# Recurrence, router and experts: experts on gathered rows of 128 in place of all tokens

## The chip, the cores and the metric

The kernel runs on one core of one Trainium2 chip, all in fp32. The time is the device time of one execution in microseconds, as the median of several runs. The engines are TensorE (PE; its weight loads are shown apart as PEld), VectorE (DVE), ScalarE (ACT), GpSimd (POOL) and SyncE (SP); DMAs are issued from SP's and POOL's queues. Each engine works through its own instructions in order.

## What is computed

```python
# hgrn2: 4 batches, 8 heads, 768 steps, head_dim 48
f = 1.0 / (1.0 + np.exp(-f_logit))
for t in range(S):
    state = f[:, :, t, :, None] * state + np.einsum('bhd,bhe->bhde', k[:, :, t], v[:, :, t])
    y[:, :, t] = np.einsum('bhd,bhde->bhe', q[:, :, t], state)
x = y.transpose(0, 2, 1, 3).reshape(B * S, H * D)          # 3072 tokens x 384
# router and experts: N, D, E, F = 3072, 384, 8, 1024
noisy_logits = x @ w_gate + np.log1p(np.exp(x @ w_noise)) * noise
top2 = np.argpartition(-noisy_logits, 2, axis=1)[:, :2]
...                                                         # top2_w: softmax of the two logits
for e in range(E):
    for k in range(2):
        mask = top2[:, k] == e
        h = np.maximum(x[mask] @ w1[e], 0.0)
        out[mask] += top2_w[mask, k, None] * (h @ w2[e])
```

Each of the 3072 tokens passes a linear recurrence, then a noisy router that picks 2 of 8 experts, and gets the weighted sum of those two experts' outputs.

## The kernel before

The sequence is cut into 6 stages of 128 steps; a stage has 4 chunks, one for each batch. `chunk` computes one: it transposes f, q and k (fp, qp, kp in L133), forms the diagonal of the attention-like matrix A (diag, L156), and goes through 7 levels. On each level PE computes scores sc (L172), DVE copies them under a mask into A (L178) and scales q (L182), and POOL scales k (kQ, L184) and forms the next decay factors T (L186); the next level's sc needs both. Then y comes from A and v (L193) and from q and the state (L197), is copied to yT (L200), and the state is renewed (kp L207, ds L214). Two chunks run in alternation, two such pairs per stage. The masks of the levels are built by POOL at the start (L91 to L96).

After a stage, `pack` re-arranges yT into xT with 10 DMAs on SP's queue (L232). `route` then computes the logits lg on PE (L244, 12 matmuls) and from them, with small operations of ACT and DVE (L249 to L272), one gate for every token and expert, which is zero for the experts that were not chosen. `expert` takes one expert and the 512 tokens of a stage, whatever the router chose: hp = w1 times xT (L295, 24 matmuls of 128x512), a ReLU on ACT (L297), yp = h times w2 (L303, 32 matmuls of 128x384), and DVE adds gate times yp to an accumulator in SBUF (L309). The last expert sends it out (L311). A matmul in fp32 shows as two records in the trace.

There are 48 pairs of expert and stage. Expert 0 on the stage before is woven into stages 1 to 5, with its instructions between the chunks' levels; the other 43 run after the last stage, expert by expert, with the weights loaded once for each expert in four DMAs of 768 KB on POOL's queue (L279, L284).

The order on each engine is made by a scheduler from the order in which the program is written and from the buffers' dependences; an engine that waits in its order holds all that stands behind.

## Time and profile before

| | us |
|---|---|
| median of 3 runs (2459.79 to 2460.49) | 2460.19 |
| span of the profiled execution | 2455.0 |
| PE busy | 2401.2 (98%) |
| DVE busy | 406.7 (17%) |
| ACT busy | 342.7 (14%) |
| POOL busy | 223.7 (9%) |

The profiled execution has the span given here; the median holds 5.2 us more, which lie around the span. Busy shares are averages over the whole span; a chain of waits tells which of the work sets the end, and the windows tell how the stages differ.

### The profile page before, as it was taken

The numbers are of one execution on the slowest core, as the hardware profiler recorded it, in microseconds if no ns is written. First come the engines' busy times: TensorE is split into PE (matmuls) and PEld (weight loads), VectorE is DVE, ScalarE is ACT, GpSimd is POOL, SyncE is SP. The second block draws the span as 40 slices with busy tenths as digits, with TensorE's granted clock in tenths as the row PEclk, the third lists the DMA queues.
The fourth block names the chain that finished last, engine by engine and source line by source line (L and its number), as shares of the span: only waits on it lengthen the run. The fifth ranks groups of instructions, "written<-read, shape, count | busy, mean of one in ns | idle before, by whom it ended". The sixth has DMA issues, their size and how long they took to land.

```text
span 2455.0 us, 23370 instructions
## 1 busy us (share of the span) xinstructions
PE 2401.2 (98%) x9984; PEld 1351.6 (55%) x9984; DVE 406.7 (17%) x777; ACT 342.7 (14%) x572; POOL 223.7 (9%) x397
## 2 busy tenths in 40 slices
PE   6999999999999999999999999999999999999999
PEld 5756666666655555555555555555555555555554
DVE  4534444443300000000000000000000000000000
ACT  1212121212120101111111111111111010101010
POOL 8322222221100000000000000000000000000000
PEclk9897979888799999999999999999999999999999
DMA  7412121211010001000100010001000100000000
GB/s 137 66 27 40 27 40 27 40 27 33 11 55 1 0 0 52 0 0 1 52 0 1 0 52 0 1 0 52 1 0 0 52 0 0 0 26 13 26 13 26
DMA packets 113255, 55.11 MB, mean 22 GB/s; under 512 B 101792, under 2 KB 104960, under 8 KB 113152
## 3 DMA queue, kind: packets, MB, share of 16 engines
q1 hardware_dynamic: 106560, 28.32, 6.8%
q0 software_dynamic: 6592, 25.29, 3.1%
q8 instruction: 79, 1.29, 0.2%
q14 instruction: 24, 0.20, 0.0%
HBM read 44.16 MB, written 4.72 MB: 20 GB/s over the span
## 4 chain that ended last, share of the span: by engine, by line
PE 95%; POOL 2%; ACT 1%; DVE 1%; issue 1%; DMA 0%; SPq 0%; ACTq 0%; DVEq 0%; POOLq 0%
PE hp L295 41%; PE yp L303 41%; PE sc L172 6%; PE y L193 2%; PE y L197 2%; PE diag L156 1%; PE lg L244 1%; PE ds L214 1%; PE fp L133 1%; PE kp L207 1%; POOL mf L94 0%; POOL mf L92 0%; PE qp L133 0%; PE kp L133 0%; DVE qP L182 0%
## 5 line engine op out<-in xcount | busy, mean ns | idle before, releaser
L295 PE MATMUL hp<-xT,w 128*128 128x512 f32 x2304 | 1016.0, 598 | 0.0
L303 PE MATMUL yp<-w,h 128*128 128x384 f32 x3072 | 1004.3, 487 | 0.0
L303 PEld LDWEIGHTS yp<-w,h 128*128 128x128 f32 x3072 | 581.6, 190 | 412.0 <-issue 21.5
L295 PEld LDWEIGHTS hp<-xT,w 128*128 128x128 f32 x2304 | 436.7, 191 | 525.6 <-issue 511.5
L297 ACT ACTIVATE h<-hp 128x512 f32<-128x512 f32 x384 | 229.3, 597 | 1672.6 <-PE hp L295 1672.6
L309 DVE SCALAR_TENSOR_TENSOR acc<-yp,gate,acc 128x384 f32<-128x384 f32 x168 | 103.8, 618 | 1628.3 <-PE yp L303 1628.3
L172 PEld LDWEIGHTS sc<-qP,kQ 48*128 48x128 f32 (+1 forms) x2688 | 185.1, 220 | 60.1 <-issue 34.3
L172 PE MATMUL sc<-qP,kQ 48*128 48x64 f32 (+1 forms) x2688 | 197.0, 309 | 19.2 <-POOL kQ L184 12.9
L178 DVE COPY_PREDICATED A<-masks,sc 128x512 f32<-128x512 uint8 x144 | 130.0, 903 | 94.3 <-PE sc L172 80.7
L279 POOL DMA_DIRECT2D w<-in_moe_w_dram x16 | 12.2, 765 | 1383.2 <-PE hp L295 1383.2
L184 POOL TENSOR_TENSOR kQ<-kQ,T 128x256 f32<-128x256 f32 x140 | 95.2, 681 | 199.3 <-PE sc L172 198.7
L182 DVE TENSOR_TENSOR qP<-qP,T 128x256 f32<-128x256 f32 x144 | 71.5, 496 | 18.0 <-PE sc L172 17.6
L193 PE MATMUL y<-A,v 128*48 128x128 f32 x384 | 50.5, 369 | 0.0
L180 ACT COPY A<-sc 64x512 f32<-64x512 f32 x24 | 13.4, 579 | 230.6 <-DVE qP L182 225.6
L197 PE MATMUL y<-qP,st 48*48 48x128 f32 x320 | 43.5, 360 | 0.0
L156 PE MATMUL diag<-qT,kQ 48*128 48x128 f32 x384 | 33.0, 306 | 9.3 <-ACT kQ L144 9.3
L186 POOL TENSOR_TENSOR T<-T 128x128 f32<-128x128 f32 (+4 forms) x140 | 36.6, 262 | 10.0
L156 PEld LDWEIGHTS diag<-qT,kQ 48*128 48x128 f32 x384 | 26.8, 201 | 16.0 <-ACT kQ L144 15.4
L193 PEld LDWEIGHTS y<-A,v 128*48 128x48 f32 x384 | 22.4, 154 | 23.7 <-issue 22.7
L158 DVE TENSOR_TENSOR A<-diag,ident 128x1024 f32<-128x1024 f32 x24 | 29.3, 1221 | 18.0 <-PE diag L156 18.0
L200 DVE COPY yT<-y 48x512 f32<-48x512 f32 x24 | 16.7, 695 | 89.2 <-ACT yT L200 89.2
L186 POOL TENSOR_TENSOR T<-f 128x256 f32<-128x256 f32 x24 | 14.7, 614 | 174.8 <-ACT f L137 174.7
(66 smaller groups left out, 468.0 us busy)
## 6 DMA issues: line engine op xcount, KB each, us to landing
w<-in_moe_w_dram POOLq DMA_DIRECT2D x32, 768.0 KB, 4.9
f<-in_f_logit_dram SPq DMA_DIRECT2D x24, 192.0 KB, 4.4
q<-in_q_dram SPq DMA_DIRECT2D x24, 192.0 KB, 5.0
k<-in_k_dram SPq DMA_DIRECT2D x24, 192.0 KB, 4.8
v<-in_v_dram SPq DMA_DIRECT2D x24, 192.0 KB, 3.3
out_dram<-acc SPq DMA_DIRECT2D x24, 192.0 KB, 1.9
xT<-yT SPq DMA_DIRECT2D x36, 96.0 KB, 2.4
xT<-yT SPq DMA_DIRECT2D x12, 64.0 KB, 2.0
```

The source lines that it names most:

```text
L156: nc.tensor.matmul(sc[:, par, cols(hp)], lhsT=kQ[rows(par), cols(hp)], rhs=qT[rows(par), cols(hp)], start=True, stop=True)
L172: nc.tensor.matmul(sc[0:nj, par, hp * HC:(hp + 1) * HC].rearrange("j (a m) -> j a m", m=m), lhsT=kQ[rows(par), hp * C:hp * C + nj], rhs=qv ...
L178: nc.vector.copy_predicated(Av, masks[:, l].rearrange("j (r x m) -> j r x m", r=2, m=m), scv)
L182: nc.vector.tensor_tensor(qv, qv, Tv[:, :, 0:1].broadcast_to((128, x, m)), ALU.mult)
L184: nc.gpsimd.tensor_tensor(kv, kv, Tv[:, :, 1:2].broadcast_to((128, x, m)), ALU.mult)
L186: nc.gpsimd.tensor_tensor(Tn, Tv[:, :, 0], Tv[:, :, 1], ALU.mult)
L193: nc.tensor.matmul(y[rows(par), par, cols(hp)], lhsT=vt[:, 2 * hp + par, :], rhs=A[:, par, cols(hp)], start=True, stop=(c == 0))
L197: nc.tensor.matmul(y[rows(par), par, cols(hp)], lhsT=state[b][rows(par), hp, :], rhs=qP[rows(par), cols(hp)], start=False, stop=True)
L295: nc.tensor.matmul(hp, lhsT=w[:, i, o:o + 128], rhs=xT[c][:, i, :], start=(i == 0), stop=(i == KO - 1))
L297: nc.scalar.activation(hs, hp, AF.Relu)
L303: nc.tensor.matmul(yp[:, 0:DM], lhsT=h[fo][:, b * C:(b + 1) * C], rhs=w2[fo // HALF][:, fo % HALF, :], start=(fo == 0), stop=(fo == FO - 1))
L309: nc.vector.scalar_tensor_tensor(a, in0=yp[:, 0:DM], scalar=g, in1=a, op0=ALU.mult, op1=ALU.add)
```

## The change

The router picks as before. Now the gates and the rows of x go to DRAM: the chunk transposes y to rows (xp, 4 transposes per chunk), and `route` writes them with the 8 gates as rows of 392 numbers to `xd` by 4 DMAs on SP's queue. `pack` is gone; lg reads yT itself (16 matmuls). A matmul pair rk with a triangle of ones counts for every chosen pair how many tokens have gone to the same expert before. From this DVE works out a place in a list per expert, and 8 indirect DMAs on POOL's queue scatter the token numbers into the lists `ids` in DRAM. `choose` decides on DVE, with some 35 small operations, which expert each of the next blocks belongs to; 55 blocks of 128 rows (LIST per stage, 22 of them after the last stage) hold all cases of 6144 chosen pairs. With the reference's inputs 52 of the 55 have rows.

`fetch` loads a block's 128 token numbers (`places`) on SP's queue, then its expert's weights in two DMAs of 1.57 MB whose address and condition come from registers (they are skipped if the buffer holds that expert), and gathers the rows of x with an indirect DMA on POOL's queue. There are three buffers of each. `block` transposes the rows (bx), computes bh (24 matmuls of 128x128), two ReLUs and by (8 matmuls of 128x384). POOL gathers the block's rows of the output, DVE adds gate times by, and POOL scatters the rows back. `clear` fills `ids`, `xd` and the output in DRAM at the start with 9 DMAs on POOL's queue, some 9.5 MB. `weave` puts the blocks of the stages before between the levels of stages 2 to 5.

The core of the diff:

```diff
...
+    LIST = [0, 9, 8, 8, 8, 22]
+    FIRST = [0, 0, 5, 0, 4, 0]
...
+    def clear():
+        nc.gpsimd.dma_start(out=ids.rearrange("(p r) o -> p (r o)", p=128), in_=free)
+        for t, w in ((out, DM), (xd, XW)):
+            for i in range(4):
+                nc.gpsimd.dma_start(out=t[i * N // 4:(i + 1) * N // 4].rearrange("(p r) d -> p (r d)", p=128),
...
+        xp = one_bank(f"xp{u}")
+        for hp in range(HP):
+            nc.tensor.transpose(xp[:, hp * 128:(hp + 1) * 128], yTc[:, hp, b, :], ident)
+        nc.scalar.copy(xrow[c][:, b, 0:DM].rearrange("t (h d) -> t h d", d=D),
+                       xp.rearrange("t (h d) -> t h d", d=DP)[:, :, 0:D])
...
-    def pack(c):
...
-                nc.tensor.matmul(lg[:, b, :], lhsT=xT[c][:, i, b * C:(b + 1) * C], rhs=w_rt[:, i, :],
+                nc.tensor.matmul(lg[:, b, :], lhsT=yTc[:, i, b, :], rhs=w_rt[:, i, :],
...
+        gates = [t([B, E], "gate0"), t([B, E], "gate1")]
+        for r in range(2):
+            nc.vector.tensor_tensor(gates[r], hot[:, r], ex[:, :, r:r + 1].broadcast_to((128, B, E)), ALU.mult)
+        nc.vector.tensor_tensor(xrow[c][:, :, XG:XG + E], gates[0], gates[1], ALU.add)
+        for b in range(B):
+            nc.sync.dma_start(out=xd[b * S + c * C:b * S + (c + 1) * C, :], in_=xrow[c][:, b, :])
+        rk = one_bank(f"rk_{c}")[:, 0:2 * B * E].rearrange("t (x b e) -> t x b e", x=2, b=B)
+        for i, w in enumerate((before, ones)):
+            nc.tensor.matmul(rk[:, i], lhsT=w, rhs=chosen, start=True, stop=True)
+        off = t([B + 1, E], "off")
+        nc.vector.tensor_copy(off[:, 0], counts[:, 0])
+        for b in range(B):
+            nc.vector.tensor_tensor(off[:, b + 1], off[:, b], rk[:, 1, b], ALU.add)
+        nc.vector.tensor_copy(counts, off[:, B:B + 1].broadcast_to((128, 2, E)))
+        place, sel, at, ati = t([B, E], "place"), t([2, B, E], "sel"), t([2, B], "at"), t([2, B], "ati", I32)
+        nc.vector.tensor_tensor(place, rk[:, 0], off[:, 0:B], ALU.add)
+        nc.vector.tensor_tensor(place, place, e_row.unsqueeze(1).broadcast_to((128, B, E)), ALU.add)
+        for r in range(2):
+            nc.vector.tensor_tensor(sel[:, r], hot[:, r], place, ALU.mult)
+        nc.vector.tensor_reduce(at, sel, AX.X, ALU.add)
+        nc.vector.tensor_copy(ati, at)
+        for b in range(B):
+            for r in range(2):
+                nc.gpsimd.indirect_dma_start(
+                    out=ids, out_offset=bass.IndirectOffsetOnAxis(ap=ati[:, r, b:b + 1], axis=0),
...
+    def choose(c):
+        L, s, g = LIST[c], FIRST[c], sum(LIST[:c])
...
+    def fetch(c, i):
+        g = sum(LIST[:c]) + i
+        w1, w2, xr, pl = w1s[g % NW], w2s[g % NW], rows_in[g % 3], places[g % 3]
+        at = nc.sync.value_load(row_no[0:1, g:g + 1], min_val=0, max_val=NID - C)
+        nc.sync.dma_start(out=pl, in_=ids[bass.ds(at, C), :])
+        r = nc.sync.value_load(load_no[0:1, g:g + 1], min_val=0, max_val=E)
+        x, go = nc.sync.snap(r & (E - 1), min_val=0, max_val=E - 1), r < E
+        for w, src in ((w1, moe_w1[bass.ds(x, 1)].rearrange("o (k p) f -> p (o k) f", p=128)),
+                       (w2, moe_w2[bass.ds(x, 1)].rearrange("o (f p) d -> p (o f) d", p=128))):
+            nc.sync.dma_start(out=w, in_=src, bounds_check="skip_entire_dma", cond=go)
+        nc.gpsimd.indirect_dma_start(
+            out=xr, out_offset=None, in_=xd,
+            in_offset=bass.IndirectOffsetOnAxis(ap=pl.bitcast(U32), axis=0), bounds_check=N - 1, oob_is_err=False)
+    def block(c, i):
+        g = sum(LIST[:c]) + i
+        w1, w2, xr, yo = w1s[g % NW], w2s[g % NW], rows_in[g % 3], rows_out[g % 2]
+        pl = places[g % 3].bitcast(U32)
+        u = f"_{g}"
+        xp = one_bank(f"bx{u}")
+        for j in range(KO):
+            nc.tensor.transpose(xp[:, j * 128:(j + 1) * 128], xr[:, j * 128:(j + 1) * 128], ident)
+        xT = ffn.tile([128, KO * 128], F32, tag="xT", name=f"xT{u}")
...
+        h = ffn.tile([128, FO, 128], F32, tag="h", name=f"h{u}")
+        for half in range(2):
+            hp = one_bank(f"bh{half}{u}")
+            for f in range(4):
+                fo = half * 4 + f
+                for j in range(KO):
+                    nc.tensor.matmul(hp[:, f * 128:(f + 1) * 128], lhsT=w1[:, j, fo * 128:(fo + 1) * 128],
+                                     rhs=xT[:, j * 128:(j + 1) * 128], start=(j == 0), stop=(j == KO - 1))
+                if f % 2:
+                    yield
+            nc.scalar.activation(h[:, half * 4:half * 4 + 4, :].rearrange("p f t -> p (f t)"), hp, AF.Relu)
+        nc.gpsimd.indirect_dma_start(
+            out=yo, out_offset=None, in_=out,
+            in_offset=bass.IndirectOffsetOnAxis(ap=pl, axis=0),
+            bounds_check=N - 1, oob_is_err=False)
+        yp = one_bank(f"by{u}")
+        for fo in range(FO):
+            nc.tensor.matmul(yp[:, 0:DM], lhsT=h[:, fo, :], rhs=w2[:, fo, :], start=(fo == 0), stop=(fo == FO - 1))
+            if fo == 3:
+                yield
+        nc.vector.scalar_tensor_tensor(yo, in0=yp[:, 0:DM], scalar=gt, in1=yo, op0=ALU.mult, op1=ALU.add)
+        nc.gpsimd.indirect_dma_start(
+            out=out, out_offset=bass.IndirectOffsetOnAxis(ap=pl, axis=0),
+            in_=yo, in_offset=None, bounds_check=N - 1, oob_is_err=False)
+        yield
...
+    def blocks(lo, hi, ready):
+        for g in range(lo, hi):
+            fetch_to(min(g + 1 + AHEAD, ready))
+            yield from block(*queue[g])
...
+    load_router()
+    clear()
+    done = 0
+    for c in range(NCH):
+        xrow[c] = wk.tile([128, B, XW], F32, tag="xrow", name=f"xrow{c}")
+        ready = sum(LIST[:c])
+        keep = 2 if c == NCH - 1 else 0
+        filler = blocks(done, ready, ready)
+        weave(c, filler, YIELDS * (ready - done - keep))
+        route(c)
+        if LIST[c]:
+            choose(c)
+            fetch_to(ready + min(1, LIST[c]))
+        for _ in filler:
+            pass
+        done = ready
+    for _ in blocks(done, NB, NB):
+        pass
...
-    for e in range(E):
-        if e:
-            w = load_expert(e)
-        for c in range(NCH) if e else (NCH - 1,):
-            by_turns(expert(e, c, *w))
...
```

Three places show how the order moves. The first is PE between two stages, from the third router call to the next stage's transposes. Before (ds is the last of the old stage):

```order
L214 MATMUL ds_3_2516<-v_3_2190,kn_3_2514 64x48 [waits Activation_49]
L214 MATMUL ds_3_2516<-v_3_2190,kn_3_2514 64x48 x7
L244 MATMUL lg_2538<-w_rt,xT_139 128x16 [waits DMAHW6_49,DMAHW7_49,DMAHW0_49,PE_49]
L133 MATMUL fp_0_2593<-ident,f_84 128x128 [waits DMAHW3_49,DVE_49]
L133 MATMUL fp_0_2593<-ident,f_84 128x128 x3
L133 MATMUL qp_0_2600<-ident,q_87 128x128 [waits DMAHW4_49,PE_49]
L133 MATMUL qp_0_2600<-ident,q_87 128x128 x3
L133 MATMUL kp_0_2609<-ident,k_90 128x128 [waits DMAHW5_49,DVE_49]
L133 MATMUL kp_0_2609<-ident,k_90 128x128 x3
```

The first lg waits for pack's DMAs, and the transposes follow at once; the other lg stand further down between them. In the change:

```order
L316 MATMUL lg_3285<-w_rt,yT_149 128x16 [waits PE_49]
L316 MATMUL lg_3285<-w_rt,yT_149 128x16 x15
L354 MATMUL rk_3344<-chosen_3323,before 128x32 [waits DVE_49,PE_49]
L354 MATMUL rk_3344<-chosen_3323,ones 128x32
L208 MATMUL fp_0_3439<-ident,f_83 128x128 [waits PE_49]
L208 MATMUL fp_0_3439<-ident,f_83 128x128 x3
L208 MATMUL qp_0_3446<-ident,q_86 128x128 x4
L208 MATMUL kp_0_3455<-ident,k_89 128x128 [waits PE_49]
```

All of lg stands together, and behind it rk, which needs `chosen` from DVE and stands ahead of the next stage's transposes.

The second is POOL in the first half of the third stage, where kQ_0 and kQ_1 are the two chunks' scaled k, level by level. Before:

```order
L184 TENSOR_TENSOR kQ_0_1761<-kQ_0_1761,f_0_1745 128x256 [waits PE_49]
L184 TENSOR_TENSOR kQ_1_1800<-kQ_1_1800,f_1_1784 128x256 [waits PE_49,Activation_49]
L184 TENSOR_TENSOR kQ_0_1761<-kQ_0_1761,T_2_0_1836 128x128x2 [waits PE_49,Pool_49]
L184 TENSOR_TENSOR kQ_1_1800<-kQ_1_1800,T_2_1_1850 128x128x2 [waits PE_49,Pool_49]
L184 TENSOR_TENSOR kQ_0_1761<-kQ_0_1761,T_2_0_1870 128x64x4 [waits PE_49,Pool_49]
L184 TENSOR_TENSOR kQ_1_1800<-kQ_1_1800,T_2_1_1884 128x64x4 [waits PE_49,Pool_49]
L184 TENSOR_TENSOR kQ_0_1761<-kQ_0_1761,T_2_0_1904 128x32x8 [waits PE_49,Pool_49]
L184 TENSOR_TENSOR kQ_1_1800<-kQ_1_1800,T_2_1_1918 128x32x8 [waits PE_49,Pool_49]
```

In the change, with the last six of the eight scatters of the stage before, of which five stand here (each DMASW wait is the one before it):

```order
L369 DMA ids<-tokens,ati_1794 27392x1 [waits DMASW2_49]
L369 DMA ids<-tokens,ati_1794 27392x1 [waits DMASW3_49]
L259 TENSOR_TENSOR kQ_0_1890<-kQ_0_1890,f_0_1874 128x256 [waits PE_49]
L259 TENSOR_TENSOR kQ_1_1924<-kQ_1_1924,f_1_1908 128x256 [waits PE_49,Activation_49]
L369 DMA ids<-tokens,ati_1794 27392x1 [waits DMASW4_49]
L259 TENSOR_TENSOR kQ_0_1890<-kQ_0_1890,T_2_0_2026 128x128x2 [waits PE_49,Pool_49]
L259 TENSOR_TENSOR kQ_1_1924<-kQ_1_1924,T_2_1_2040 128x128x2 [waits PE_49,Pool_49]
L369 DMA ids<-tokens,ati_1794 27392x1 [waits DMASW5_49]
L259 TENSOR_TENSOR kQ_0_1890<-kQ_0_1890,T_2_0_2077 128x64x4 [waits PE_49,Pool_49]
L259 TENSOR_TENSOR kQ_1_1924<-kQ_1_1924,T_2_1_2091 128x64x4 [waits PE_49,Pool_49]
L259 TENSOR_TENSOR kQ_0_1890<-kQ_0_1890,T_2_0_2155 128x32x8 [waits PE_49,Pool_49]
```

The kQ steps have moved behind scatters, one or two between each pair of levels. In the tail POOL's row reads for each block: gather of output rows, gather of the rows of the block after next but one, scatter.

```order
L480 DMA rows_out_156<-out_dram,places_182 128x384 [waits DMASW6_49]
L447 DMA rows_in_155<-xd,places_184 128x392 [waits DMAHW2_49,DMASW1_49,PE_49]
L490 DMA out_dram<-rows_out_156,places_182 3072x384 [waits DMASW7_49,DVE_49]
L480 DMA rows_out_157<-out_dram,places_183 128x384 [waits DMASW1_49]
L447 DMA rows_in_153<-xd,places_182 128x392 [waits DMAHW5_49,DMASW3_49,PE_49]
L490 DMA out_dram<-rows_out_157,places_183 3072x384 [waits DMASW2_49,DVE_49]
```

Each gather of output rows waits (DMASW) for the scatter before it, and each scatter for DVE.

The third is SP in the third stage, with the loads of the second pair of chunks (f, q, k, v). Before they stand in a row:

```order
L127 DMA v_2_2132<-in_v_dram 128x8x48 [waits DMAHW7_49,PE_49]
L124 DMA f_86<-in_f_logit_dram 128x8x48 [waits DMAHW0_49,PE_49]
L124 DMA q_89<-in_q_dram 128x8x48 [waits DMAHW1_49,PE_49]
L124 DMA k_92<-in_k_dram 128x8x48 [waits DMAHW2_49,PE_49]
L124 DMA f_84<-in_f_logit_dram 128x8x48 [waits DMAHW3_49,PE_49]
L124 DMA q_87<-in_q_dram 128x8x48 [waits DMAHW4_49,PE_49]
L124 DMA k_90<-in_k_dram 128x8x48 [waits DMAHW5_49,PE_49]
L127 DMA v_3_2190<-in_v_dram 128x8x48 [waits DMAHW6_49,PE_49]
L124 DMA f_85<-in_f_logit_dram 128x8x48 [waits DMAHW7_49,PE_49]
```

In the change:

```order
L441 DMA places_182<-ids 128x1 [waits DMASW6_49,DMAHW4_49,DMASW4_49,DMASW0_49]
L446 REGISTER_ALU
L446 ISA
L446 DMA w_0_163<-in_moe_w_dram 128x3x1024 [waits DMAHW5_49,PE_49]
L446 REGISTER_ALU
L446 ISA
L446 DMA w_0_166<-in_moe_w_dram 128x8x384 [waits DMAHW6_49,PE_49]
L195 DMA v_3_2617<-in_v_dram 128x8x48 [waits DMAHW7_49,PE_49]
L195 DMA v_0_2656<-in_v_dram 128x8x48 [waits DMAHW0_49,PE_49]
L192 DMA f_84<-in_f_logit_dram 128x8x48 [waits DMAHW1_49,PE_49]
L192 DMA q_87<-in_q_dram 128x8x48 [waits DMAHW2_49,PE_49]
L192 DMA k_90<-in_k_dram 128x8x48 [waits DMAHW3_49,PE_49]
```

The loads stand behind a `places` load, which waits for the scatter of the block that used that buffer (DMASW), and behind two weight loads, which wait for PE.

## Rows read from the trace of the kernel before

**Rows 1.** The page's chain that ended last: shares by engine and by line.

```profile
PE 95%; POOL 2%; ACT 1%; DVE 1%; issue 1%; DMA 0%; SPq 0%; ACTq 0%; DVEq 0%; POOLq 0%
PE hp L295 41%; PE yp L303 41%; PE sc L172 6%; PE y L193 2%; PE y L197 2%; PE diag L156 1%; PE lg L244 1%; PE ds L214 1%; PE fp L133 1%; PE kp L207 1%; POOL mf L94 0%; POOL mf L92 0%; PE qp L133 0%; PE kp L133 0%; DVE qP L182 0%
```

**Rows 2.** The chain in time: start us, us, what, with records.

```profile
698.54 20.64 PE yp L303 x64
719.18 20.60 PE hp L295 x48
```

**Rows 3.** Windows: length, busy by engine (x instructions), clock, DMA share, GB/s.

```profile
core 0: us, PE busy (x) PEld busy (x) DVE busy (x) ACT busy (x) POOL busy (x), PEclk, DMA share, GB/s
0.00:22.00 22.00, 13.88 (x88) 11.28 (x88) 8.37 (x17) 4.82 (x7) 21.34 (x23) 1.00 1.32 147
...
328.00:444.00 116.00, 111.46 (x904) 74.59 (x904) 50.38 (x102) 24.06 (x41) 28.35 (x56) 0.87 0.21 35
...
560.00:681.00 121.00, 114.73 (x871) 75.62 (x872) 47.59 (x95) 22.16 (x37) 24.46 (x48) 0.85 0.11 21
681.00:2455.00 1774.00, 1770.26 (x4811) 913.54 (x4810) 109.34 (x198) 209.85 (x351) 19.69 (x26) 1.00 0.04 15
```

**Rows 4.** The chain in time: transposes at clock 1.00, and the router's matmuls.

```profile
619.44 0.44 PE qp L133 x4
...
105.59 2.15 PE lg L244 x20
```

**Rows 5.** The page's groups: line, engine, names, count | busy us, mean ns.

```profile
L309 DVE SCALAR_TENSOR_TENSOR acc<-yp,gate,acc 128x384 f32<-128x384 f32 x168 | 103.8, 618 | 1628.3 <-PE yp L303 1628.3
```

**Rows 6.** The page's DMA issues, and the DMA view: KB, us to landing.

```profile
w<-in_moe_w_dram POOLq DMA_DIRECT2D x32, 768.0 KB, 4.9
f<-in_f_logit_dram SPq DMA_DIRECT2D x24, 192.0 KB, 4.4
...
xT<-yT SPq DMA_DIRECT2D x12, 32.0 KB, 2.0
noise<-in_moe_noise_dram POOLq DMA_DIRECT2D x4, 24.0 KB, 5.2
w_rt<-in_moe_w_gate_dram POOLq DMA_DIRECT2D x1, 12.0 KB, 4.4
```

**Rows 7.** POOL by line, whole span, and the chain's first pieces.

```profile
L92 POOL TENSOR_SCALAR_AFFINE_SELECT mf<-mf 128x512 f32<-128x512 f32 x6 | 10.8, 1796 | 0.0
L94 POOL TENSOR_SCALAR_AFFINE_SELECT mf<-mf 128x512 f32<-128x512 f32 x6 | 10.7, 1790 | 0.0
L96 POOL CAST masks<-mf 128x512 uint8<-128x512 f32 x6 | 3.9, 651 | 0.0
L108 POOL DMA_DIRECT2D noise<-in_moe_noise_dram x4 | 3.4, 844 | 0.0
L91 POOL MEMSET mf<- 128x512 f32 x6 | 3.2, 528 | 0.0
...
30.53 0.06 POOL kQ L184
...
45.68 7.11 PE sc L172 x64
```

**Rows 8.** Timeline behind the last lg: start us, us, engine, line, operation.

```profile
681.32 0.20 ACT L249 ACTIVATE sp<-lg 128x32 f32<-128x32 f32 x1 [12.45 <-PE lg L244]
681.53 1.28 ACT L250 ACT_TABLE_LOAD   x1
...
685.11 0.19 DVE L252 SCALAR_TENSOR_TENSOR sp<-lg,sp 128x32 f32<-128x32 f32 x1 [15.52 <-ACT sp L251]
...
687.28 0.18 DVE L269 TENSOR_TENSOR hot<-iota,fx 128x32 f32<-128x32 f32 x1
```

**Rows 9.** Windows: one microsecond of a weight load.

```profile
949.00:950.00 1.00, 1.00 (x4) 0.57 (x3) 0.00 (x0) 0.00 (x0) 0.00 (x0) 1.00 1.05 434
```

**Rows 10.** The chain in time: the second pair of stage 0; state matmuls.

```profile
60.41 0.67 PE ds L214 x16
...
95.44 0.71 DVE yT L200
...
659.29 0.60 PE y L197 x4
```

More of the change, by code (lines that the diff above doesn't have):

```diff
@@ new lines @@
+    used = ctile([2, E], "used")
+    nc.vector.memset(counts, 0.0)
+    nc.vector.memset(used, 0.0)
+    experts = ctile([NW + NB], "experts")
+    nc.vector.memset(experts, -1.0)
+    load_no = ctile([NB], "load_no", I32)
+    picks = [ctile([LIST[c], E], f"picks{c}") if LIST[c] else None for c in range(NCH)]
+    row_no = ctile([NB], "row_no", I32)
+    places = [ctile([1], f"places{i}", I32) for i in range(3)]
+    zero = wk.tile([128, N // 128 // 4 * XW], F32, tag="zero", name="zero", bufs=1)
@@ L317, in by_turns, with chunks, weave @@
+    def chunks(c, bs):
+        for b in bs:
+            yield from chunk(c, b)
+            load_to(c * B + b + 1 + NLD)
+    def weave(c, filler, n):
+        turns, done, t = 2 * (NL + 3 - (c == NCH - 1)), 0, 0
+        streams = [chunks(c, range(0, B, 2)), chunks(c, range(1, B, 2))]
         while streams:
```

252 lines of the change are left out of this document (161 added, 91 removed).

## The prediction

> **What bounds the kernel now.** I read the page's shares and its chain first: TensorE (PE) is busy 98% of the span, and of the chain that ended last 82% is two lines, hp and yp [rows 1]. The reader is to see that no wait stands in this chain, so only PE work that goes away pays. The chain in time gives the unit: one expert on 512 tokens is 20.60 us of hp (48 records, 0.429 each) and 20.64 of yp (64 records, 0.3225 each), 41.24 together [rows 2]; 48 such units are 1980 us. The windows then split the span: a woven stage lasts 116 us with a granted clock of 0.87, and from 681 us on PE does nothing but experts, at clock 1.00 [rows 3]. So the recurrence costs 116 - 41.24 = 74.8 us a stage, and the experts' time is proportional to rows.
>
> **What is removed.** 24,576 row-expert pairs (8 experts x 3072) become 55 x 128 = 7,040. On PE that is 55 quarter-units for 192.
>
> **What one block costs.** bh has 24 matmuls of 128 columns, 48 records; by has 8 of 384 columns, 16 records; bx has 3 transposes. by: 16 x 0.3225 = 5.16 us [rows 2]. bh does not occur before: every weight load now feeds 128 columns for 512. Bounds: the transposes load 128x128 weights and stream 128 columns, four in 0.44 us, 0.110 each [rows 4], so load and stream overlap; the router's matmuls, which are almost only weight load (16 columns), take 2.15 us for 20, 0.1075 each [rows 4], of which 0.094 is left for the load when 16 x 0.429/512 is taken off. If load and stream stood one behind the other, a record would be 0.094 + 0.107 = 0.201. I take 0.110, the row nearest in shape: 48 x 0.110 = 5.28. bx adds 0.33. In the tail bx of the next block follows by at once, but its copy to SBUF stands on VectorE (DVE) behind the block's output operation (0.618 us for 128x384 [rows 5]): twice 0.62, less the 0.33 that bx covers, is about 0.95 of PE idle. One block: 10.77 + 0.95, say **11.75 us**; 55 are 646. So PE's expert work falls by about 1330 us. What follows takes some 230 of it back.
>
> **L, the unknown.** The trace has no DMA that takes addresses from a list. The change has 48 scatters of token numbers, and a gather of rows, a gather of output rows and a scatter per block, all on GpSimd's (POOL's) queue. From issue to landing I take **L = 4.4 us**, the 12 KB w_rt load from the same queue; the bounds are 2.0 (the 32 KB xT copy) and the longest of that queue in kind, noise with 5.2 [rows 6], and above that I go to 8, since each DMA has 128 separate rows and its list must be read first.
>
> **The start.** POOL's work is the chain until 45.68 us [rows 7]. In the new order POOL has all masks, two memsets of 2.1 us (4 x 0.528, by the 128x512 memset), five of 0.4, constants, 8 router loads and 9 DMAs of clear before the first kQ; 17 x 0.84 (the noise issue) = 14.3 [rows 7]. With the masks' 28.6 (10.8 + 10.7 + 3.9 + 3.2) it ends at about 52, where the first kQ stood at 30.53 [rows 7]: **+21**, all on the path.
>
> **A stage boundary.** rk now stands on PE right behind lg and ahead of the next transposes; its input comes 6.4 us after lg: 681.32 is where ScalarE (ACT) starts, with table loads of 1.28, and the second hot ends at 687.46 [rows 8]. Before, PE had other work there; now the in-order PE stops: **6.6** with the last sum. What is queued behind it is the whole next stage. lg is 32 records for 24 (+0.8) and xp 16 transposes (+1.8); pack's 10 DMAs go. Then POOL: each of the 8 scatters waits for the one before, and kQ of level 0 stands behind the fourth, level 1 behind the fifth, and so on. The first goes out about 10.5 after lg (6.6 and some 18 DVE operations of 0.19 [rows 8]); kQ of level 0 may go at 10.5 + 3 x 4.4 = 23.7, where its data is there at about 12.5: **11** late, and the later levels do not catch up. PE has no block in hand in that half of the stage, so nothing covers it.
>
> **Blocks in a stage.** Four come in a lump after the first pair of chunks, the rest among the second pair's levels. On SyncE's (SP's) queue the loads of the second pair stand behind the fetch of a block that waits for block 3's scatter: 0.62 + 4.4 + three issues of about 1 + the load's 4.4 [rows 6], 13 us, with a little bh work over it: **12**. Output gathers among the kQ steps cost POOL up to L each for 4 blocks, 0 to 18; I take **4**, since 11.75 us of block work lies between them.
>
> **The weights.** On the reference's inputs the 55 blocks hold 52 with rows, and each loads its 3.15 MB: a block finds another expert than the one before it in its buffer, so the skip saves next to nothing. At 434 GB/s, read in one microsecond of a w load [rows 9], that is 7.2 us in a block of 11.75, with three buffers: hidden. The cover is gone below 268 GB/s.
>
> **The sum**, ends of each stage's lg. Stage 0: its last copy ended at 96.15 [rows 10], + 21 + 1.8 + 3.4 = 122. Stage 1 has no blocks: twice the pair of 35.7 us (60.41 to 96.15 [rows 10]) + 9.6 for 64 state records of 0.15 [rows 10] + 6.6 + 1.8 + 11 + 3.4 = 104, to 226. Stage 2: 74.8 + 2.6 + 6.6 + 11 + 12 + 4 + 9 x 11.75 = 217, to 443. Stages 3 and 4 with 8 blocks: 205 each, to 853. Stage 5: 121 - 41.24 [rows 3] less 2.7 of pack's wait, 77 + 36.2 + 6 x 11.75 = 184, to 1037; its other two blocks run in the seam. The seam: 10.5 + 8 x 4.4 + 2.4 + 4.4 = 53 from lg to the first bx of the tail, over which those two blocks (24 us) lie, to 1090. Tail 22 x 11.75 = 258.5, the last output operation and scatter 5: 1353. The span before is 2455.0 and the median 5.2 more; so **1358, rounded to 1360**.
>
> **Rivals.**
> - *Weight loads not hidden* under 128 columns: 0.201 for 0.110, 48 x 0.091 x 55 = +240, **1600**. For it: no matmul of before has streams as short as its loads with full weights, since hp's loads hide beneath 0.43 us. Against it: the transposes. 10%. [...]
> - *The rows' chain sets the pace.* In the tail the gather of output rows waits for the last block's scatter, and the next scatter for it: 2L + 0.9 per block, 9.7 with 4.4. From L = 5.5 it is longer than 11.75. L = 6 gives 1.2 x 22 + 1.6 x (9 in the seam, 4 chunk loads) + 5 boundaries x 7 = +80, **1440**; L = 8: +300, **1660**. For it: nothing of the sort is in the trace; against: 5.2 is the longest small load of this queue [rows 6]. 17%.
> - *Weights bound the blocks.* The first 22 us moved 147 GB/s [rows 3] with small packets; at that rate a block needs 21.4 us: 22 x 9.7 + 4 x 3 x 9.7 = +330, **1690**. Against: rows of 1.5 and 4 KB as in before's w loads. 5%.
> - *Fast lists*, L = 2.0: boundaries -7 each, seam -22, chunk loads -10: **1290**. 4%.
> - *Slower.* One place: POOL's queue, whose three listed DMAs per block and eight per boundary stand one behind the other. At 2L + 0.9 for 55 blocks, 7L at five boundaries and 9L in the seam, 2460 is reached from L of about 12.5: then PE waits for POOL in every block, and the time is **2500**. For it: the list length, 128 entries. Against: it is almost three times every row of this queue. 3%. [...]
>
> **How the numbers follow.** The forecast with L of 2.5 to 5.5, own range 1300 to 1430, has 61%. The range 1270 to 1550 adds the fast lists, two thirds of the rows' chain and half of the unhidden loads (those that hide in part); some 19% is left out above. Faster 0.97; within 0.2%, about what a measurement can tell from no change, 0.005; slower 0.025.
>
> **What would show it.** In the changed kernel's trace: bh at 0.11 us a record and a tail period of 11.75; lg to rk with PE idle 6.6; kQ late behind scatters; L in the list of DMA issues; PE idle about 29 us after the blocks of the seam; first kQ at 52. Wrong makes it a bh record near 0.2, a tail period of 2L + 0.9 over 12, or w landing later than 24 us after its issue.

## The result and the profile after

The changed kernel takes 1335.09 us (1324.47 to 1338.07, four runs) against 2460.34, a ratio of 0.5421 (95% interval 0.5401 to 0.5441). The prediction was 1360 with 1270 to 1550. The profiled execution has a span of 1332.4 us; what lies around it is 1.7 us in that run, where 5.2 was assumed. One run further below, of 1348.62 us, was in a slower state than the others and is left out of its kernel's median.

Set against the sum of the prediction, by the end of each router's lg (stage 0 is the first stage):

| part | predicted us | measured us | difference |
|---|---|---|---|
| stage 0 with the start | 122 | 117.6 | -4 |
| stage 1, no blocks | 104 | 114.6 | +11 |
| stage 2, 9 blocks | 217 | 202.1 | -15 |
| stage 3, 8 blocks | 205 | 193.5 | -12 |
| stage 4, 8 blocks | 205 | 194.8 | -10 |
| stage 5, 6 blocks | 184 | 163.4 | -21 |
| seam, with 2 blocks | 53 | 52.7 | 0 |
| tail of 22 blocks and end | 263 | 293.7 | +31 |

That the total comes so near is in part luck: single parts are off by up to 31 us, and their errors, of both signs, cancel to -20. The windows of the changed kernel at those bounds answer to [rows 3] (length, busy time by engine with instructions, PEclk, DMA share, GB/s):

```profile
...
117.60:232.20 114.60, 93.71 (x821) 77.40 (x820) 50.11 (x111) 21.06 (x36) 36.49 (x64) 0.59 0.23 36
...
434.30:627.80 193.50, 168.83 (x1357) 135.15 (x1356) 67.19 (x180) 30.31 (x53) 61.11 (x88) 0.85 0.54 176
...
1038.70:1332.40 293.70, 254.59 (x1474) 200.92 (x1474) 28.57 (x88) 26.27 (x44) 66.11 (x65) 0.96 0.62 226
```

PE was 98% busy and is 84% busy now. The granted clock, 1.00 in the long expert part before, averages 0.59 in the stage without blocks, 0.85 in a stage with eight, and 0.96 in the tail.

The page and the DMA view give the work itself (for the DMA rows: KB where shown, and the median us from issue to landing):

```profile
PE 1119.6 (84%) x8461; PEld 905.7 (68%) x8461; DVE 399.5 (30%) x1046; ACT 189.0 (14%) x322; POOL 428.4 (32%) x602
...
L475 PE MATMUL bh<-xT,w 128*128 128x128 f32 x2640 | 340.0, 291 | 47.8 <-DVE xT L460 47.1
...
w<-in_moe_w_dram SPq DMA_DIRECT2D x110, 1536.0 KB, 9.1
...
rows_in<-xd,places POOLq DMA_INDIRECT x55, 6.1
rows_out<-out_dram,places POOLq DMA_INDIRECT x55, 4.1
out_dram<-rows_out,places POOLq DMA_INDIRECT x55, 2.7
ids<-tokens,ati POOLq DMA_INDIRECT x48, 3.8
```

A weight load lands 9.1 us after its issue (median), and the profile lists no wait of PE for one. The listed DMAs land after 2.7 to 6.1 us, in the range of 2.0 to 8 that was given to L; taken was 4.4. PE's waits by releaser (us in total, times, longest):

```profile
PE sc L247 <- POOL kQ L259: 58.6, 16, 26.5
PE bh L475 <- DVE xT L460: 47.1, 39, 3.8
PE rk L354 <- DVE sm L341: 29.9, 5, 6.0
PE bx L458 <- DMA rows_in<-xd,places: 24.2, 5, 19.7
PE sc L247 <- DVE A L233: 20.7, 11, 4.0
```

This list is the map for all that follows: the first four entries are terms of the prediction; the last, the diagonal's copy A, is not in it.

### The profile page after: what moved, and what is told of

It reads as the page before. It is cut to its first block, busy times and chain, and to the rows that moved or that the text cites. A ratio compares the mean times of both kernels' runs of the same rounds, so it can differ in the third digit from the quotient of the medians.

```text
span 1332.4 us, 21528 instructions
## 1 busy us (share of the span) xinstructions
PE 1119.6 (84%) x8461; PEld 905.7 (68%) x8461; DVE 399.5 (30%) x1046; ACT 189.0 (14%) x322; POOL 428.4 (32%) x602
## 3 DMA queue, kind: packets, MB, share of 16 engines
q1 hardware_dynamic: 186096, 187.32, 43.8%
## 5 line engine op out<-in xcount | busy, mean ns | idle before, releaser
L475 PE MATMUL bh<-xT,w 128*128 128x128 f32 x2640 | 340.0, 291 | 47.8 <-DVE xT L460 47.1
L475 PEld LDWEIGHTS bh<-xT,w 128*128 128x128 f32 x2640 | 324.7, 204 | 61.5 <-DVE xT L460 56.3
L247 PE MATMUL sc<-qP,kQ 48*128 48x64 f32 (+1 forms) x2688 | 241.4, 354 | 82.1 <-POOL kQ L259 58.6
L486 PE MATMUL by<-w,h 128*128 128x384 f32 x880 | 293.8, 487 | 0.0
L486 PEld LDWEIGHTS by<-w,h 128*128 128x128 f32 x880 | 162.9, 190 | 102.2
L490 POOL DMA_INDIRECT out_dram<-rows_out,places x55 | 56.1, 1021 | 391.6 <-DVE rows_out L489 333.8
L479 ACT ACTIVATE h<-bh 128x512 f32<-128x512 f32 x110 | 65.7, 597 | 628.6 <-PE bh L475 628.6
L466 DVE TENSOR_TENSOR gw<-picks,rows_in 128x8 f32<-128x8 f32 (+2 forms) x71 | 10.5, 166 | 377.0 <-DMA rows_in<-xd,places 377.0
L369 POOL DMA_INDIRECT ids<-tokens,ati x48 | 48.1, 1003 | 165.4 <-DVE have L393 70.5
L489 DVE SCALAR_TENSOR_TENSOR rows_out<-by,gt,rows_out 128x384 f32<-128x384 f32 x55 | 33.9, 616 | 197.7 <-PE by L486 182.4
L480 POOL DMA_INDIRECT rows_out<-out_dram,places x55 | 56.7, 1031 | 111.6 <-DMA out_dram<-rows_out,places 107.1
L447 POOL DMA_INDIRECT rows_in<-xd,places x55 | 56.2, 1022 | 92.2 <-DMA places<-ids 64.5
L257 DVE TENSOR_TENSOR qP<-qP,T 128x256 f32<-128x256 f32 x144 | 75.3, 523 | 19.4 <-PE sc L247 17.2
L458 PE MATMUL bx<-ident,rows_in 128*128 128x128 f32 x165 | 29.9, 293 | 24.8 <-DMA rows_in<-xd,places 24.2
```

The costliest lines, as they stand in the source:

```text
L247: nc.tensor.matmul(sc[0:nj, par, hp * HC:(hp + 1) * HC].rearrange("j (a m) -> j a m", m=m), lhsT=kQ[rows(par), hp * C:hp * C + nj], rhs=qv ...
L257: nc.vector.tensor_tensor(qv, qv, Tv[:, :, 0:1].broadcast_to((128, x, m)), ALU.mult)
L447: nc.gpsimd.indirect_dma_start(out=xr, out_offset=None, in_=xd, in_offset=bass.IndirectOffsetOnAxis(ap=pl.bitcast(U32), axis=0), bounds_ch ...
L458: nc.tensor.transpose(xp[:, j * 128:(j + 1) * 128], xr[:, j * 128:(j + 1) * 128], ident)
L475: nc.tensor.matmul(hp[:, f * 128:(f + 1) * 128], lhsT=w1[:, j, fo * 128:(fo + 1) * 128], rhs=xT[:, j * 128:(j + 1) * 128], start=(j == 0), ...
L479: nc.scalar.activation(h[:, half * 4:half * 4 + 4, :].rearrange("p f t -> p (f t)"), hp, AF.Relu)
```

## The block and the tail

A regular block of the tail (timeline: start us, us, engine, line, operation, idle before and its releaser):

```profile
1067.20 0.52 PE L458 MATMUL bx<-ident,rows_in 128*128 128x128 f32 x3 [1.41 <-DMA rows_in<-xd,places]
...
1068.50 5.62 PE L475 MATMUL bh<-xT,w 128*128 128x128 f32 x48 [0.79 <-DVE xT L460]
...
1073.96 5.33 PE L486 MATMUL by<-w,h 128*128 128x384 f32 x16
```

From bh's start to by's it is 5.46 us, 0.114 for each of the 48 records; by's 16 take 5.17, to the next bx at 1079.13. The 1.30 us from bx to bh (1.34 in the next blocks) are the output operation (0.62) and the copy of xT (0.55), one behind the other on DVE. From bx to bx regular blocks take 11.93 to 12.00 us, where 11.75 was predicted. With 0.114 a record, near the 0.110 of the transposes in [rows 4], the weight loads are hidden beneath 128 columns; the rival of 0.201 a record has fallen.

But the first two blocks take 15.0 and 13.5 us, four more 15.7 to 16.6 and three about 13. One of the four:

```profile
1103.05 0.49 PE L458 MATMUL bx<-ident,rows_in 128*128 128x128 f32 x3
...
1106.15 0.17 DVE L466 TENSOR_TENSOR gw<-picks,rows_in 128x8 f32<-128x8 f32 x1 [12.71 <-DMA rows_in<-xd,places]
1106.23 0.61 DVE L489 SCALAR_TENSOR_TENSOR rows_out<-by,gt,rows_out 128x384 f32<-128x384 f32 x1
1106.76 0.55 DVE L460 COPY xT<-bx 128x384 f32<-128x384 f32 x1
...
1107.36 7.25 PE L475 MATMUL bh<-xT,w 128*128 128x128 f32 x48 [3.81 <-DVE xT L460]
```

```profile
1104.00:1106.00 2.00, 0.00 (x0) 0.00 (x0) 0.00 (x0) 0.00 (x0) 0.00 (x0) 1.00 1.01 393
...
1108.00:1110.00 2.00, 2.00 (x11) 2.00 (x11) 0.00 (x0) 0.00 (x0) 0.14 (x1) 0.50 0.66 246
```

bx of this block ran at 1103.05; its rows were there. DVE, however, had the gate product of the *next* block (gw, L466) in its order ahead of this block's copy of xT, and that product waited until 1106.15 for its gathered rows. Behind it stood the output operation (L489) and the copy (L460), and behind the copy all of bh. While PE paused, the DMA engines moved 393 GB/s; two weight loads had been issued at 1098.04 and the gather of the rows at 1099.99. Behind the pause the granted clock was 0.50 for some 3 us, and bh took 7.25 instead of 5.62. The wait was 3.0 us longer than a regular block's 0.85, and the block cost 4.6 us more. In the three blocks of about 13 us bh waited 1.7 to 2.1 us and was not slowed (5.62 each).

## The first half of a stage

In a stage with blocks, the first half is a different kernel from the second. Three windows of stage 3 of the table (columns as above):

```profile
434.30:480.00 45.70, 28.90 (x251) 27.22 (x250) 27.52 (x96) 9.21 (x14) 20.07 (x33) 0.58 0.25 45
480.00:549.00 69.00, 63.76 (x420) 46.75 (x419) 9.91 (x32) 9.03 (x16) 15.31 (x16) 0.85 0.83 308
549.00:627.80 78.80, 76.18 (x693) 61.18 (x690) 29.75 (x52) 12.08 (x23) 25.73 (x39) 1.00 0.45 137
```

In the first window there are no blocks: PE is 63% busy at a clock of 0.58. Then, from 490.23 on, four blocks come in a lump, then blocks and levels mixed at 1.00. What happens at the start of that first window (timeline of several engines):

```profile
440.32 0.60 PE L354 MATMUL rk<-chosen,before 128*128 128x32 f32 x2 [5.99 <-DVE sm L341]
...
443.68 0.98 POOL L369 DMA_INDIRECT ids<-tokens,ati  x1 [10.88 <-DVE have L393]
...
457.57 1.06 POOL L369 DMA_INDIRECT ids<-tokens,ati  x1 [3.27 <-DMA ids<-tokens,ati]
458.66 1.63 POOL L259 TENSOR_TENSOR kQ<-kQ,f 128x256 f32<-128x256 f32 x2
...
459.55 3.68 PE L247 MATMUL sc<-qP,kQ 48*128 48x64 f32 x32 [3.36 <-POOL kQ L259]
```

rk waits 5.99 us (6.6 predicted). The first of the eight scatters goes out at 443.68, the fourth at 457.57, 4.6 us from one to the next, and kQ of level 0 stands behind the fourth: it goes at 458.66, 24.4 us after lg ended at 434.3. The prediction had 23.7. PE's waits for kQ are 6.5 us in this stage, and 3.9 more are for the diagonal's copy A on DVE, which stood behind the small operations of `choose`. The two together come near the 11 that was predicted for kQ alone; the copy was not in the prediction.

## The experiments

Two questions were at stake. In the tail, theory **A** is that the rows arrive late because 3.15 MB of weights per block move beside them, and that the order on DVE carries this to PE; theory **B** is that the listed DMAs are slow of themselves, since each waits for the one before. At the boundaries the question is whether the chain of eight scatters costs the time, or (theory **C**) rk and DVE. From the third run on, "theory A" in an expectation means the theory that it states there itself. All kernels below are timed against the kernel before in the same session; for the changed kernel compare 1335.

**Weights loaded once.**

```diff
-            nc.sync.dma_start(out=w, in_=src, bounds_check="skip_entire_dma", cond=go)
+            if g < NW:
+                nc.sync.dma_start(out=w, in_=src, bounds_check="skip_entire_dma", cond=go)
```

> Left out: the weight loads of all blocks but the first three, so later blocks multiply with the weights that lie in the buffers; all else is as in the changed kernel (1335 us). Theory A: the tail's four blocks of about 16 us (the others take 11.96) come from the weights' 3.15 MB per block, behind which the row gathers land after a median of 6.1 us; DVE's order (the gate product of a later block ahead of the output operation and of the copy of xT) carries that to PE, and the clock falls with the pause. Then the gathers land in 2 to 3.5 us, no tail block is over 12.5, the tail falls from 293.7 to about 268 and the time to 1295 to 1315. Theory B: the listed DMAs are late by themselves, since each waits for the one before. Then the gathers stay near 6 us and the time stays within 1325 to 1345.

1304.9 us (1299.75 to 1309.76). The row gathers (DMA view):

```profile
rows_in<-xd,places POOLq DMA_INDIRECT x55, 3.2
```

3.2 us for 6.1, and after the tail's first block (14.4) all 20 that follow take 11.96 on average, none over 12.0. The tail is 271.8 us for 293.7. Theory A holds for the tail. The weights' traffic, for which no wait of PE is listed, costs 30 us by the medians; of the 24 between the two profiled executions, 22 are the tail.

**Gate product behind the output operation.**

```diff
-        gw, gt = ffn.tile([128, E], F32, tag="gw", name=f"gw{u}"), ffn.tile([128, 1], F32, tag="gt", name=f"gt{u}")
+        gg = ffn.tile([128, E + 1], F32, tag="gw", name=f"gw{u}", bufs=1)
+        gw, gt = gg[:, 0:E], gg[:, E:E + 1]
```

> One edit: gate product and its sum share one tile with one buffer, so that on DVE a later block's product stands behind the output operation and the xT copy. Weights are loaded as before. Theory A: the gathers stay at about 6 us, but no tail block waits for them: 11.96 throughout, 20 us less in the tail, 1310 to 1320 in all. If instead PE in those blocks waits for the rows of the very next block (theory B), the pauses move from bh to bx and the time stays within 1325 to 1345.

1322.73 us (1319.33 to 1328.67): 12 less, not 20, and between the ranges of the two theories. The tail is 285.5 us; its first three blocks take 13.7 to 14.7, and further on one of 15.2 and one of 16.5 remain. In the longest another gather is late:

```profile
1231.36 0.62 DVE L490 SCALAR_TENSOR_TENSOR rows_out<-by,gw,rows_out 128x384 f32<-128x384 f32 x1 [13.48 <-DMA rows_out<-out_dram,places]
```

Now the output operation (L490 here) itself waits, for the gather of output rows, and the copy of xT stands behind it; bh waits 3.71 us and takes 7.25. So the mechanism is the order on DVE, but a late gather finds a second place in it.

**One scatter of eight.**

```diff
             for r in range(2):
+                if (b, r) != (0, 0):
+                    continue
                 nc.gpsimd.indirect_dma_start(out=ids, ...
...
-    nc.gpsimd.memset(free, BIG)
+    nc.gpsimd.iota(free, pattern=[[1, NID // 128]], base=0, channel_multiplier=22)
```

> Left out: seven of the eight scatters of token numbers in each stage; the lists are filled with valid token numbers at the start, so that every block still gathers and scatters 128 rows. Theory A: the chain of eight scatters (4 to 5 us each) sets the first half of each stage: kQ stands behind it, no block can start, and PE's granted clock is 0.58 there. Without it the blocks start in the first half, the clock there rises, a stage with 8 blocks falls from 194 to some 165, the seam from 52.7 to about 28: 1170 to 1230. Theory C: the first half is set by DVE (choose and the diagonal's copies) and by rk; then only kQ's waits of 5 to 7 us per boundary and the seam's 20 go: 1280 to 1290.

1269.42 us (1266.48 to 1272.96): 66 less, more than C allows and less than A promised. The same stage as above, now 180.0 us for 193.5, with the blocks starting in the first half (the first bx 27 us after lg, where it was 56):

```profile
409.70:455.00 45.30, 31.70 (x224) 27.40 (x224) 22.51 (x93) 10.43 (x16) 12.70 (x23) 0.70 0.74 252
455.00:524.00 69.00, 65.22 (x585) 52.48 (x583) 22.57 (x50) 12.07 (x22) 25.59 (x38) 0.98 0.71 240
...
```

The seam, from lg to the tail's first bx, falls from 52.7 to 35 us, stage 1 loses 7 and stages 2 to 5 lose 49 together, while the tail is 8 longer. The first window is still at 0.70 with 31.7 of 45.3 us busy: there rk, the small operations of DVE and the first gather remain, which is C's part. Both are at work: the chain of scatters is worth 66 us here, and what C's part is worth alone no run measured. The lists of this kernel name other rows than the router chose, and what that changes in the gathers is not known apart from their landing time (6.0 us for 6.1).

**Clear and router loads on ACT's queue.**

```diff
-                nc.gpsimd.dma_start(out=w_rt[par * DP:par * DP + D, :, i * E:(i + 1) * E], in_=wr[par])
+                nc.scalar.dma_start(out=w_rt[par * DP:par * DP + D, :, i * E:(i + 1) * E], in_=wr[par])
...
-        nc.gpsimd.dma_start(out=ids.rearrange("(p r) o -> p (r o)", p=128), in_=free)
+        nc.scalar.dma_start(out=ids.rearrange("(p r) o -> p (r o)", p=128), in_=free)
...
```

> One edit: the 8 router loads and the 9 DMAs of clear are issued from ACT's queue and not from POOL's. Theory A: they stand ahead of the first kQ with 0.55 to 0.85 each, so the first kQ goes at about 34 instead of 45.6, the first lg ends at about 106 instead of 117.6, and the time falls by 10 to 13, to 1322 to 1325. Rival: PE then waits for the masks or for the first loads instead, and the gain is under 4.

1330.96 us (1327.76 to 1340.21, three runs): 4 less, which cannot be told from no change, since the runs of the changed kernel alone spread from 1324 to 1338. In the profile the first lg ended at 112.5 for 117.6, so about half of the gain was there. PE's wait for kQ at the start, 26.5 us, became two others:

```profile
PE qp L208 <- ACT f L212: 16.1, 1, 16.1
PE fp L208 <- DMA f<-in_f_logit_dram: 12.3, 2, 7.7
```

The 17 issues now stand on ACT ahead of the first sigmoid, which starts at 33.49 us. From 17.2 to 28.36 ACT issued nothing; next in its order was the DMA that fills `ids`, which needs the buffer that POOL fills at 25.85. The queue was changed, not the place.

**Four blocks held back, first attempt.** These three kernels tested something else than was meant: the first fetch of the next list was written ahead of the held blocks, so four held blocks and one more were fetched into three buffers before the first was used.

```diff
-        keep = 2 if c == NCH - 1 else 0
+        keep = 4 if ready > done else 0
```

> One number: in every stage that has blocks (not only in the last, and four for two) the last four blocks are held back and written behind the router, ahead of the next stage. Theory A (a stage's first half waits for the lists, since no block is at hand): PE works on four held blocks, about 48 us, while the eight scatters run (10.5 + 8 x 4.5 = 46), at three boundaries and in the seam; kQ's and the diagonal's waits there (7 to 12 us) go, the blocks of the next list can start in the first half, where the clock was 0.58, and the seam's 20 us of idle PE go. rk's 6 us stay. 193.5 to about 180 per stage with 8 blocks: 1265 to 1290 for 1335. Rival: the work is only moved, since PE is the bound anyway, and only the seam's 20 us are won: 1310 to 1320.

1511.85 us (1507.51 to 1515.95).

```diff
-        route(c)
+        ranked = route(c)
+        for _ in range(YIELDS):
+            next(filler, None)
+        ranked()
```

> As the kernel that holds back four blocks, and the first of the four is written between the choice of the experts and the count rk. Theory: rk's input is there when the block ends, so the 6 us at three boundaries and in the seam are covered; the scatters start about 6 us later, which three more blocks (36 us) nearly cover: 15 to 25 us less than with four held blocks alone. Rival: the later scatters cost as much as rk's wait gave, within 5 us of it.

1502.6 us (1497.85 to 1506.61).

> Four edits together: gate product behind the output operation, xT copy on ACT, split router with four held blocks, and the router loads and clear issued from POOL in the middle of stage 0 and not ahead of its first kQ. By the theories the gains add, apart from the long tail blocks, which two of them mend: split router about 1255, less 35 for the tail and the pauses, less 10 at the start: 1195 to 1225. If they collide on DMA (the weights' 3.15 MB per block then meet faster blocks): 1230 to 1260.

1448.26 us (1445.13 to 1454.72). Nothing on the theories follows from these three, since their blocks worked on overwritten buffers and waited for each other's fetches; what follows is that with the next list's first fetch ahead of the held blocks three buffers allow two of them, the number that the change has.

**The copy of xT on ACT.**

```diff
-        nc.vector.tensor_copy(xT, xp[:, 0:KO * 128])
+        nc.scalar.copy(xT, xp[:, 0:KO * 128])
```

> One edit: the copy of xT from PSUM is done by ACT and not by DVE. Theory: in each of some 40 blocks the pause between bx and bh (1.08 us from the end of by's last to bh in the tail, since the copy stands behind the output operation on DVE) falls to about 0.6, and the copy no longer stands behind a later block's gate product that waits for its rows, so the tail's blocks of 16 us go too: tail period 11.5 throughout, 1290 to 1305. Rival: the output operation, itself behind the product, holds PSUM banks, and the long blocks stay: 1315 to 1325.

1337.57 us (1329.46 to 1345.49): the rival's mechanism, but no gain at all, where the rival too had 10 to 20 us. The regular period is 11.74 for 11.96 (11.5 was expected), and a late gather reaches PE by a third way:

```profile
1192.65 0.17 DVE L466 TENSOR_TENSOR gw<-picks,rows_in 128x8 f32<-128x8 f32 x1 [13.18 <-DMA rows_in<-xd,places]
1192.73 0.61 DVE L489 SCALAR_TENSOR_TENSOR rows_out<-by,gt,rows_out 128x384 f32<-128x384 f32 x1
...
1193.45 7.09 PE L486 MATMUL by<-w,h 128*128 128x384 f32 x16 [2.10 <-issue]
```

gw waited for its rows until 1192.65, the output operation stood behind it, and by of the next block started at 1193.45, 0.11 us after that operation ended. The profile names no releaser here; that by waited for the PSUM bank that the output operation reads is inferred from these times. The 16 records then took 7.09 us for 5.33; from 1195 to 1197 us the granted clock was 0.50.

**Four blocks held back, with the fetch behind them.**

```diff
         for _ in filler:
             pass
         done = ready
+        if LIST[c]:
+            fetch_to(ready + 1)
```

> The edit of holding back four blocks again, now with the first fetch of the next list written behind the held blocks. In the first attempt it stood ahead of them, so that all four held blocks were fetched into three buffers before the first was used: those blocks worked on overwritten rows and weights, and PE waited 214 us for rows. Theory A: PE works on the held blocks, about 48 us, while the eight scatters run, at three boundaries and in the seam; kQ's and the diagonal's waits there go, the next list's blocks start in the first half of the stage, where the clock was 0.58, and the seam's 20 us of idle PE go: 1265 to 1290 for 1335. Rival: the held blocks' gathers and scatters stand on POOL between the eight scatters and are held up by them, and only the seam gains: 1310 to 1335.

1379.25 us (1377.14 to 1380.4): 44 *more*, worse than the rival too. POOL, SP and PE in the seam:

```profile
1032.86 0.97 POOL L369 DMA_INDIRECT ids<-tokens,ati  x1 [3.68 <-DMA ids<-tokens,ati]
1034.13 0.99 POOL L490 DMA_INDIRECT out_dram<-rows_out,places  x1 [0.30 <-issue]
...
1045.20 0.97 POOL L369 DMA_INDIRECT ids<-tokens,ati  x1 [2.65 <-DMA ids<-tokens,ati]
...
1051.54 1.05 POOL L447 DMA_INDIRECT rows_in<-xd,places  x1 [5.37 <-DMA places<-ids]
```

```profile
1048.73 0.36 SPq L441 DMA_DIRECT2D places<-ids  x1
```

```profile
SPq L441 <- DMA ids<-tokens,ati: 8.8, 1, 8.8
```

```profile
1057.49 0.87 PE L458 MATMUL bx<-ident,rows_in 128*128 128x128 f32 x3 [18.14 <-DMA rows_in<-xd,places]
```

The held blocks' own listed DMAs stand in POOL's order between the eight scatters (L369), each of which waits 2 to 4 us for the one before: the scatter of a held block (L490, 1034.13) went between the fifth and the sixth. That is the rival, but the larger cost lies on SP. The third held block is fetched only while the held blocks run. Its load of `places` reads `ids`, into which the eight scatters write, and it went at 1048.73, 3.5 us after the eighth had been issued; SP's wait for that scatter is the 8.8 us shown. The gather of the rows then waited for this load and went at 1051.54, and PE waited 18.14 us for the rows. At the three other boundaries it is the same: the load 2.9 to 3.3 us behind the eighth scatter, and PE idle for 16.5 to 19.1 us. The work meant to cover the chain reads the buffer that the chain writes, although the entries it needs had long been there.

> As the run before, and the first of the four held blocks is written between the choice of the experts and the count rk. Theory: rk's input is there when the block ends, so its 6 us at three boundaries and in the seam are covered; the scatters start about 6 us later, which three more blocks (36 us) nearly cover: 15 to 25 us less than with four held blocks alone. Rival: the later scatters cost as much as rk's wait gave, within 5 us of it.

1380.73 us (1376.56 to 1384.16), the same as without the split: the rival. PE's wait for rk at the boundaries fell from 30.0 to 12.0 us, while its waits for rows rose from 75.9 to 93.3 and for A from 32.3 to 49.1.

**Three edits together.** The gate product behind the output operation, xT on ACT, and:

```diff
-    load_router()
-    clear()
...
             t += 1
+            if c == 0 and t == turns // 2:
+                load_router()
+                clear()
```

> Three edits together: the gate product behind the output operation on DVE (alone 1323), the xT copy on ACT (alone no gain: a late row gather still held the output operation, and with it PSUM), and the router loads and clear issued from POOL in the middle of stage 0. Theory: with both DVE edits a late gather holds neither the output operation nor the xT copy, so the tail runs at its period of 11.73 without long blocks (260 us from its first bx instead of 293.7), and the first kQ no longer stands behind 17 DMA issues (first lg ends 6 to 10 us earlier): 1285 to 1300. Rival: the gather of output rows, also late behind the weights, holds the output operation as before and PSUM with it, and long blocks of 14 to 16 us remain: 1310 to 1320.

1293.51 us (1292.57 to 1296.79), a ratio of 0.5266 (0.5257 to 0.5275): faster than the changed kernel by 41.6 us, and the fastest kernel here that computes all of it. The first lg ends at 104.4 us for 117.6. The tail takes 271 us for 293.7, with a period of 11.74: of the 19 periods after the first two, one is a us or more above that (13.15); in the changed kernel seven are clearly above the regular 11.96. Neither of the two edits for the tail alone did this (12 us and nothing). What PE still waits for:

```profile
PE sc L247 <- POOL kQ L259: 43.8, 27, 7.5
...
PE sc L247 <- DVE A L233: 27.1, 15, 4.3
PE bx L458 <- DMA rows_in<-xd,places: 22.9, 7, 17.6
```

**The count rk later.** As before, and rk, the scatters and `choose` written behind the next stage's first transposes.

```diff
-        route(c)
-        if LIST[c]:
-            choose(c)
...
+        ranked = route(c)
+        def lists(c=c, ranked=ranked, ready=ready):
+            ranked()
+            if LIST[c]:
+                choose(c)
...
+            if t == 1:
+                first()
```

> As the run before, and the count rk with the scatters and the choice of blocks is written after the next stage's first transposes and not ahead of them (not in the last stage). On PE rk stands behind the first diagonal, on POOL kQ of level 0 goes before the first scatter. Theory: rk's wait of 6.0 us at five boundaries is covered by the transposes, and kQ's and the diagonal's waits there (7 to 12 us) shrink by some 5, since the first levels no longer stand behind four scatters: 30 to 50 us less than the run before. Rival: the lists are ready later by as much, the blocks start later, and a stage's end moves little: within 15 us of the run before.

1312.91 us (1308.88 to 1314.36): 19 more than without. The rival was right in kind and too mild:

```profile
PE bx L464 <- DMA rows_in<-xd,places: 58.3, 10, 17.6
PE sc L247 <- POOL kQ L259: 25.8, 29, 8.5
...
PE sc L247 <- DVE A L233: 9.3, 9, 2.2
```

rk's 30.0 us are gone (11.8 came back as waits of qp for DVE), kQ's waits fell from 43.8 to 25.8 and A's from 27.1 to 9.3, together 66 us. The waits of bx for rows rose from 22.9 to 58.3, and PE's mean clock fell from 0.848 to 0.814 in the profiled executions. In this kernel the lists are the chain that decides when blocks can start; the waits that were taken away at the boundary by letting the lists start later came back as waits for rows.

## Why the prediction was right, and where it was not

- **PE's work** fell nearly in proportion to the rows (0.33 of the experts' busy time for 0.29 of the pairs), and in the tail the 128-column matmuls ran near the transposes' rate (0.114 us a record for 0.110): 11.96 us a block for 11.75. This step is the 1330 us of which 1125 remained, and it held: PE was busy with hp and yp for 2020 us before, and is for 664 with bx (29.9), bh (340.0) and by (293.8).

```profile
L295 PE MATMUL hp<-xT,w 128*128 128x512 f32 x2304 | 1016.0, 598 | 0.0
L303 PE MATMUL yp<-w,h 128*128 128x384 f32 x3072 | 1004.3, 487 | 0.0
```

- **The start**: the first kQ at 45.63 us for 52. Half of this is the size of POOL's 17 issues: they took 0.53 to 0.88 us, 11.0 in sum for 14.3. The end of the first lg is 4 us early.
- **rk, scatters, seam**: 5.99 for 6.6; kQ of level 0 after 24.4 us for 23.7; 52.7 for 53 in the seam, with PE idle for 19.7 and 5.9 us in it, where about 29 was predicted. L was mis-sized in its parts (ids 3.8, out scatter 2.7, out gather 4.1, row gather 6.1 us for 4.4), not in its mean.
- **The loads of chunks, 12 us per stage: the step failed.** It read the buffer names wrongly, as the section on the change does where it calls them loads of the second pair. The loads that stand behind a fetch on SP go into the buffers that the second pair's transposes have just freed, so they are the next stage's:

```profile
548.85 0.60 PE L208 MATMUL fp<-ident,f 128*128 128x128 f32 x4
```

```profile
554.83 0.72 SPq L192 DMA_DIRECT2D f<-in_f_logit_dram  x1
```

The transposes (fp) ran at 548.85, without a wait, and the f load that the fetch held went out at 554.83. PE's only waits for such loads, 5.3 us, are in stage 0. In stages 2 to 5 this term alone is 48 of the 57 us by which they were overestimated; the other 9 were not traced by a run.
- **Stage 1**, 11 us longer: without blocks its granted clock averages 0.59, while the pair of stage 0 from which it was scaled ran at 0.69 in its window of the kernel before (60 to 99 us). PE's waits for rk, kQ and A in it, 18.3 us, are what was predicted for a boundary (17.6), so the difference is in PE's busy time. That the clock makes it is argued; no run changed the clock there by itself.
- **The weights: the step was incomplete.** That they are hidden from PE is right. That they lie in the way of the 200 KB row gathers (6.1 us to landing, 3.2 with the weights loaded once), and that DVE's order lets a gather for one block stop the block before it (3.81 us before the bh shown), was not in the sum. Against the regular period it makes some 21 of the tail's 31 us; the first block, whose bh took 8.48 us for 5.62 behind the seam's wait of 19.7 (the granted clock was 0.50 from 1039 to 1046), makes 3, the period of 11.96 for 11.75 makes 5, and the end the rest. With the weights loaded once the tail was 22 us shorter.

Three of the rivals name things that are there in small: late rows that hold PE (seven tail blocks), weights in the way (30 us), and POOL's queue (66 us for seven scatters of eight). The chain of the rows' rival, output gather and scatter, never set the tail's period: with 4.1 and 2.7 us and the 0.9 between it is 7.7 of 11.96, and what held PE was the row gather beside the weights. That rival's +300 for L = 8 does not follow from its own terms, which scaled from L = 6 give about 240; nothing in the forecast hangs on it.

## What to carry to other kernels

Replacing work for all rows by gathered work paid here nearly in proportion to the rows (0.33 of the experts' PE time for 0.29 of the pairs), since a block's bh and by took 10.63 us in the tail and a quarter of an expert's 512 tokens 10.31 before; what is lost here goes to the lists, so look first which in-order queue, and which buffer, the lists share with other work. The weight loads, for which no wait of PE is listed, still cost 30 us here, by delaying small transfers: the row gathers landed after a median of 6.1 us beside them and 3.2 without. So look for instructions of a later block that stand in an engine's order ahead of the present one. Moving a wait off one engine without shortening the chain behind it gave nothing, or a loss, four times here (ACT's queue, xT alone, held blocks, the later count).
